# A four-layer transformer kernel on one core: x turned on TensorE instead of in the DMA, and some reciprocals spread over the partitions through DRAM

## The chip, the cores and the metric

The kernel runs on one core of one Trainium2 chip. A core has a matrix engine (TensorE, PE in the profile; PEld is its weight load), a vector engine (VectorE, DVE), an activation engine (ScalarE, ACT), GpSimd (POOL), a sync engine (SP) that here only issues transfers, and 16 DMA engines. SBUF is the working memory with 128 partitions, PSUM takes what TensorE writes in 8 banks of 512 floats per partition, and DRAM lies outside. The metric is the device time of one execution in microseconds (us).

## The reference

Input x has 2048 tokens of 1024 features in bf16. Four layers follow: A, B, A, B. Each is a residual: x = x + layer(normalise(x)). The normalisation takes mean and variance over the features, without weights. There are 32 heads of 32 features.

- Layer A is linear attention. q, k, v come from one weight matrix. q and k are multiplied per head by a 32 x 32 matrix `w_phi`; phi of the result p is softmax(p) and softmax(-p) side by side (64 features). Per head, kv is the sum over all tokens of phi_k times v, and z the sum of phi_k. The output is (phi_q kv) / (phi_q z + 1e-6), and it goes through the matrix `wo`.
- Layer B is full softmax attention with 32 heads over 2048 x 2048 scores, then its own `wo`.

```
pq = einsum(q, w_phi); phi_q = [softmax(pq), softmax(-pq)]      # and phi_k alike
kv = einsum(phi_k, v);  z = sum(phi_k)
o  = (phi_q @ kv) / (phi_q @ z + 1e-6);  x = x + o @ wo          # layer A
o  = softmax(q k^T / sqrt(32)) @ v;      x = x + o @ wo          # layer B
```

## The kernel before

**Layout.** x is kept turned in SBUF for the whole run as `xT`: features on the partitions, tokens along the free side, eight blocks of 128 features by 2048 tokens. The tokens are worked in four chunks of 512 (c = 0 to 3). A group g stands for 128 features, four heads.

**Planner.** The program is not written in its order. The builder makes a list of operations (`op` and `dma`), each with an engine, a duration in the planner's reckoning, the operations it depends on, its buffers and a priority; `Sched.run` then plays them out in a simulated time and gives the order in which they are emitted. Smaller priority numbers come first. A transfer is reckoned to land 2 us plus its `kb`/200 after its issue, where half of the second part also holds up the transfers behind it (`RING`), plus a `slack` of its own. Buffers lie in one SBUF arena (`SBUF_ARENA` bytes per partition) and in the PSUM banks; `QUOTA` says how many of a class may live at once. `TIE` seeds a small random change of the reckoned durations. Many constants are due times (`LATER`, `VQ`, `KP`, `OUT`, `QA`, `AK`, `EARLY` and more), which shift the priority of a piece of work. Each engine takes its instructions in the emitted order.

**Start.** `load_x` brings x. Chunk 0: blocks 0 to 3 by four transposing transfers on SP's queue, blocks 4 to 7 by two plain transfers on POOL's queue into `xnat`, 16 products with the identity on TensorE, and two copies out of PSUM on VectorE. Chunks 1 to 3 come by transposing transfers on SP. `fold_phi` folds `w_phi` into the key weights: weights come plainly (`wnat`, first half by one 1 MB transfer on ACT's queue, second half by four on SP's), TensorE turns them (line 748), four heads at a time are multiplied by the block-diagonal `phi` (line 530, tile `phi_t`), and ACT and VectorE copy the result to a slab (lines 781 and 784). The query weights are folded later, from transposing transfers. `phi_t` is a tile of its own, zeroed by the first instruction of VectorE and filled by four transfers on POOL's queue (line 1380).

**Layer A.** `layernorm` squares x (lines 635 on VectorE for the first chunk, 640 on ACT), sums over the features with a matrix of ones on TensorE (line 602 or 530), spreads the means (line 619) and normalises on VectorE (lines 683 to 695). `a_keys` makes phi_k and v per 128 tokens and sums kv and z over all four chunks. Then `a_queries` runs for each chunk and each half of the heads (hf): query products (530), two exponentials (951), sums over each softmax (962), logarithms, their difference and exponential (968 to 974: the ratio of the two softmax sums, called w here), w spread to all partitions and multiplied onto the second half (979), numerators (994, copied by ACT in 1002), denominators (1009), and the reciprocal of the denominators by logarithm and exponential (1014, 1016). The reciprocal has one useful row per head: rows 32a to 32a+3 hold four heads of group a. `split_hl` splits it on VectorE into a bf16 part and a remainder (915, 916), `spread` multiplies with the 0/1 matrix `selr` on TensorE so that each row fills 32 partitions (931), and line 1020 multiplies the numerators with the spread reciprocal out of PSUM into `oc`. `selb` does the same for w. `a_out` multiplies with `wo` and adds to `xT` (1033). The first of the chunk's later work is planned so that the next chunk's queries come between.

**Layer B.** `attention` computes scores (1257) in groups of three 128 x 512 units, takes the exponential on ACT (1273), and multiplies with v and with ones (1305). For some pairs of units (`COUNT`, `PAIRS`, `HOST`) `exp_dve` computes the exponential on VectorE in six instructions (1184 to 1203); its buffers are `x` (class xy), `z` (xz), `u` (xx) and `y` (xu). The denominators take a way through DRAM: 1362 stores the reciprocals to `rd`, 1364 reads them back with each of four rows broadcast to 32 partitions. Projections for later groups (`b_k`, `b_v`, `b_q`, `b_o`) fill TensorE between. Near the end of the first layer B the keys of the second layer A begin.

Of the kernel before, what the change touches and what calls it, by code (L numbers as in the profile page):

```python
# [55 lines left out]
TIE = 17  # L56
# [13 lines left out]
class Sched:  # L70
# [99 lines left out]
    def run(self):  # L170
# [32 lines left out]
        while left:  # L203
# [108 lines left out]
SBUF_ARENA = 172 * 1024 - 256  # L312
# [3 lines left out]
LONG = {"kT", "v", "slab", "slabk", "xn", "xn1", "kvacc", "kvm", "zm", "wnat"}  # L316
MODEST = {"slabk", "xn1", "e1", "vp1", "pkf", "lnw1", "w2o"}
NUMS = 2
LATER = ((26.4, 16.7, 25.9, 7.3), (18.7, 27.9, 15.9, 13.5))
VQ = (((0, 7.1), (50.5, 3.1), (53.0, 8.9)), ((15.5, 8.4), (75.8, 14.1), (152.2, 9.9)))  # L320
FULL = 5
OUT = (35.9, 27.1)
EARLY = (2.0, 4.0)
DUE = 0.0
BOOST = 25.0
EVAC = 30.0
QA = (105.3, 4.5)
# [4 lines left out]
         "rs": 8, "pkf": 1, "cden": 2, "part": 8, "w2r": 1,  # L332
# [8 lines left out]
HOST = ((), (16,), (11, 17), (0, 11, 21), (4, 10, 17, 24))  # L341
SIDE = (2, 4)
FEW = (((0, 1, 3), (0, 1, 2)), ((0, 1, 3), (0, 1, 2)))
WHOLE = 2
WK = (0.0, 1.5)
SLABD = (1, 3)
TOK = (0.0, 0.6, 0.61, 0.62)
SLOW = 6.0
HALF = 4
KGAP = (6.2, 2.2)  # L350
LATE = 15.3
KP = (0, 39.1, 45.7, 92.0, 62.9, 125.6, 160.1, 205.2)
BO = 225
OP0 = (240.8, 265.9, 289.4)
OGAP = (2.0, 2.6, 1.9)
COUNT = ((0, 0, 1, 2, 4, 4, 4, 3, 4, 3, 3, 4, 4, 4, 4, 3, 4, 3, 3, 4, 3, 2, 1, 2, 0, 2, 4, 2, 1, 2, 3, 3),
    (2, 4, 5, 4, 4, 4, 3, 5, 4, 4, 4, 4, 4, 4, 5, 4, 3, 5, 4, 4, 4, 4, 4, 4, 4, 2, 5, 4, 3, 1, 4, 4))
PAIRS = ((), ((0, 2),), ((0, 2), (1, 2)), ((0, 1), (0, 5), (1, 3)), ((0, 1), (0, 5), (1, 1), (1, 5)),
    ((0, 1), (0, 3), (0, 6), (1, 1), (1, 5)), ((0, 1), (0, 3), (0, 6), (1, 1), (1, 3), (1, 6)))
AK = ((0, 201.9), (1, 231.9), (2, 260.5))  # L360
OUT1 = ((177.6, 3.1), (195.5, 1.0), (246.4, 1.0))


def act_us(n):
    return n / 1200 + 0.064
# [10 lines left out]
def kernel(  # L376
# [52 lines left out]
    phi_t = const.tile([P, G * P], BF16, tag="phi")  # L429
    nc.vector.memset(phi_t[:].bitcast(U32), 0)  # L430
# [45 lines left out]
    gone = []  # L476
    qd = dram_p.tile([P, 2 * G * C512], BF16, tag="qd")
# [78 lines left out]
    def load_x():  # L556
        nb, nv = sb("xnat", TB, C512)
        nat = [dma(-24.0, lambda h=h: nc.gpsimd.dma_start(
            out=nv()[:, 2 * h:2 * h + 2, :],
            in_=A_x[0, 2 * h * P:2 * h * P + 2 * P, C512:D].rearrange("(t p) f -> p t f", p=P)),  # L560
            (), [nb], q="GQ", kb=256, issue=0.75) for h in range(2)]
        for lo, hi, prio, us, kb in ((0, 1, -24.0, 1.3, 128), (1, 2, -9.0, 1.3, 400), (2, NC, -8.0, 2.0, 800)):
            last = []
            for po in range(PO if lo else PO // 2):
                last.append(dma(
                    prio, lambda lo=lo, hi=hi, po=po: nc.sync.dma_start_transpose(
                        out=xT[:, po, lo * C512:hi * C512], in_=A_x[0, lo * C512:hi * C512, po * P:(po + 1) * P]),
                    issue=us, kb=kb))
                if not lo:
                    last[-1].slack = 0.5  # L570
            for pr in () if lo else ((4, 5), (6, 7)):
                tb, tv = ps("wt", ANY)

                def tr(pr=pr, tv=tv, h=0):
                    o = tv().bitcast(BF16)
                    for po in pr:
                        for t in (2 * h, 2 * h + 1):
                            nc.tensor.transpose(
                                out=o[:, (po % 2 * TB + t) * P:(po % 2 * TB + t + 1) * P],
                                in_=nv()[:, t, (po - 4) * P:(po - 3) * P], identity=ident[:])  # L580
                t1 = None
                for h in range(2):
                    t1 = op("PE", 4 * 0.11, lambda tr=tr, h=h: tr(h=h), [nat[h], t1], [tb, nb], -17.0, mode="n")
                last += [op("DVE", 0.69, lambda pr=pr, tv=tv: nc.vector.tensor_copy(
# [1008 lines left out]
```

## Time and profile before

| what | value |
|---|---|
| median of 3 runs | 2245.05 us (2242.07 to 2246.89) |
| profiled execution, its time | 2247.36 us |
| its span, first to last instruction | 2245.1 us |
| granted TensorE clock, mean | 0.998 |
| busy: PE, ACT, DVE, POOL | 2176.1, 1985.7, 1855.9, 197.0 us |
| exponentials of layer B on ACT (line 1273) | 1366 instructions, 1668.5 us |
| the same on VectorE (line 1203, one per pair of units) | 209 instructions, 254.7 us |
| DMA moved | 119.67 MB |

A row of a group has line, engine, operation, the tiles written and read, shape, count, then busy time and mean duration in ns, then idle time of the engine just before and what ended it. PE's busy time counts overlapping matmuls once; it does not say that the matmuls run at their best rate. A row of the timeline has start and duration in us, engine, line, operation and count. SPq, POOLq and ACTq are the queues in which an engine issues transfers. In the table by stage, each engine has its busy time and instruction count.

### The profile page before, as it was taken

The numbers are of one execution on the slowest core, as the hardware profiler recorded it, in microseconds if no ns is written. First come the engines' busy times: TensorE is split into PE (matmuls) and PEld (weight loads), VectorE is DVE, ScalarE is ACT, GpSimd is POOL, SyncE is SP. The second block draws the span as 40 slices with busy tenths as digits, with TensorE's granted clock in tenths as the row PEclk, the third lists the DMA queues.
The fourth block names the chain that finished last, engine by engine and source line by source line (L and its number), as shares of the span: only waits on it lengthen the run. The fifth ranks groups of instructions, "written<-read, shape, count | busy, mean of one in ns | idle before, by whom it ended". The sixth has DMA issues, their size and how long they took to land.

```text
span 2245.1 us, 82636 instructions
## 1 busy us (share of the span) xinstructions
PE 2176.1 (97%) x36788; PEld 872.2 (39%) x36788; DVE 1855.9 (83%) x2761; ACT 1985.7 (88%) x1939; POOL 197.0 (9%) x299
## 2 busy tenths in 40 slices
PE   7999999999999999999999999999999999999999
PEld 4554454444333333333333444433333333333333
DVE  7986873698899889677887788799999999988968
ACT  4436669999999999999998555999999999999998
POOL 1110000000001010121124200000000000100000
PEclk9999999999999999999999999999999999999999
DMA  9220101111122221222235100111111100211111
GB/s 207 49 81 3 33 24 42 41 34 34 51 57 88 74 73 54 64 96 73 78 110 152 59 5 10 36 37 38 36 29 29 35 24 19 73 31 35 47 36 38
DMA packets 121789, 119.67 MB, mean 53 GB/s; under 512 B 57752, under 2 KB 99800, under 8 KB 121432
## 3 DMA queue, kind: packets, MB, share of 16 engines
q1 hardware_dynamic: 102392, 56.64, 10.0%
q0 software_dynamic: 17424, 56.18, 8.7%
q8 instruction: 287, 4.70, 0.9%
q10 hardware_dynamic: 1616, 1.57, 0.2%
q14 instruction: 70, 0.57, 0.1%
HBM read 79.23 MB, written 14.14 MB: 42 GB/s over the span
## 4 chain that ended last, share of the span: by engine, by line
PE 28%; ACT 23%; DVE 9%; issue 5%; DMA 1%; SPq 0%; ACTq 0%; DVEq 0%
ACT arena L1273 22%; PE psum L530 14%; PE psum L1305 6%; PE psum L1257 6%; DVE arena L1203 2%; DVE arena L1184 1%; DVE arena L1196 1%; DVE arena L1201 1%; DVE arena L1193 1%; ACT arena L823 1%; DMA arena<-arena 1%; DVE arena L1370 1%; DVE arena L1198 1%; DVE arena L1057 1%; PE psum L994 0%
## 5 line engine op out<-in xcount | busy, mean ns | idle before, releaser
L1273 ACT ACTIVATE arena<-psum 128x1536 bf16<-128x1536 f32 (+1 forms) x1366 | 1668.5, 1446 | 12.0 <-PE psum L1257 7.1
L530 PE MATMUL psum<-arena 128*32 128x512 bf16 (+1 forms) x18432 | 1058.3, 358 | 12.5 <-DVE arena L836 2.7
L530 PEld LDWEIGHTS <-arena 128*32 128x32 bf16 x18944 | 459.8, 96 | 447.2 <-issue 175.7
L1305 PE MATMUL psum<-arena 128*32 128x512 bf16 x4096 | 628.1, 383 | 4.0 <-issue 2.0
L1305 PE MATMUL psum<-arena,ones_bf 128*32 128x512 bf16 x4096 | 628.1, 383 | 0.0
L1257 PE MATMUL psum<-arena 32*128 32x512 bf16 x4096 | 536.2, 383 | 27.2 <-ACT arena L1273 22.4
L1257 PEld LDWEIGHTS <-arena 32*128 32x128 bf16 x4096 | 158.4, 91 | 555.8 <-issue 549.0
L1184 DVE TENSOR_SCALAR arena<-psum 128x512 int32<-128x512 f32 x418 | 284.5, 686 | 101.7 <-PE psum L1257 90.3
L1203 DVE SCALAR_TENSOR_TENSOR arena<-arena 128x1024 int16<-128x1024 int32 x209 | 254.7, 1218 | 5.7 <-DVE arena L1201 0.4
L1305 PEld LDWEIGHTS <-arena 128*32 128x32 bf16 x4096 | 163.2, 95 | 227.8 <-issue 177.0
L1305 PEld LDWEIGHTS <-ones_bf 128*32 128x32 bf16 x4096 | 161.3, 95 | 22.3 <-issue 7.9
L705 POOL DMA_DIRECT2D arena<-in_B_wqkv_dram x46 | 42.2, 919 | 1248.6 <-PE psum L530 302.5
L1193 DVE TENSOR_SCALAR arena<-arena 128x1024 f16<-128x1024 int16 x209 | 143.8, 690 | 4.4 <-DMA arena<-arena 0.3
L1196 DVE TENSOR_TENSOR arena<-arena 128x1024 f16<-128x1024 f16 x209 | 142.6, 684 | 4.6
L1201 DVE TENSOR_TENSOR arena<-arena 128x1024 f16<-128x1024 f16 x209 | 142.6, 684 | 3.1
L1057 DVE CAST arena<-psum 128x512 bf16<-128x512 f32 x128 | 87.7, 685 | 57.6 <-PE psum L530 57.3
L823 ACT ACTIVATE arena<-psum 128x512 bf16<-128x512 f32 x80 | 43.0, 596 | 82.6 <-PE psum L530 66.7
L827 DVE TENSOR_REDUCE arena<-arena 128x32 f32<-128x1024 bf16 x64 | 77.0, 1214 | 33.3 <-ACT arena L823 33.2
L530 PE MATMUL psum<-xT,onesD 128*32 128x512 bf16 x1144 | 103.1, 381 | 1.3 <-DVE arena L836 0.7
L1321 DVE COPY arena<-psum 128x512 f32<-128x512 f32 x126 | 86.3, 685 | 15.4 <-PE psum L1305 15.0
L1198 DVE TENSOR_SCALAR arena<-arena 128x1024 f16<-128x1024 f16 x209 | 87.9, 422 | 1.7
L836 DVE TENSOR_TENSOR arena<-psum,arena 128x1024 bf16<-128x1024 f32 x64 | 77.4, 1219 | 13.3 <-PE psum L530 9.7
(124 smaller groups left out, 1383.6 us busy)
## 6 DMA issues: line engine op xcount, KB each, us to landing
arena<-rd SPq DMA_DIRECT2D x62, 256.0 KB
arena<-in_B_wqkv_dram POOLq DMA_DIRECT2D x58, 256.0 KB, 4.1
arena<-in_B_wo_dram POOLq DMA_DIRECT2D x40, 256.0 KB, 4.4
arena<-arena SPq DMA_DIRECT2D x256, 32.0 KB
arena<-wd_k POOLq DMA_DIRECT2D x32, 256.0 KB, 5.0
arena<-in_A_wqkv_dram POOLq DMA_DIRECT2D x32, 256.0 KB, 4.6
arena<-arena SPq DMA_DIRECT2D x96, 64.0 KB
arena<-arena SPq DMA_DIRECT2D x248, 2.0 KB
```

Of the source, the lines that this page charges most:

```text
L530: nc.tensor.matmul(out_[ks, :], lhsT=lhsT[:, ks], rhs=rhs, start=start, stop=stop, tile_position=(0, 32 * k), skip_group_check=True)
L1057: return op("DVE", dve_us(512), lambda: nc.vector.tensor_copy(out=dst(), in_=src()), [dep], bufs, prio)
L1184: o = op("DVE", dve_us(512), lambda: nc.vector.tensor_scalar(out=x_v()[:, k, :].bitcast(I32), in0=s_v()[:, x * C512:(x + 1) * C512], scala ...
L1193: last = op("DVE", 1024 / 1920 + 0.15, lambda: nc.vector.tensor_scalar(out=z(), in0=x_v().bitcast(I16).rearrange("p a (n two) -> p a n two ...
L1196: last = op("DVE", 1024 / 1920 + 0.15, lambda: nc.vector.tensor_tensor(out=u(), in0=z(), in1=z(), op=ALU.mult), [last], [z_b, u_b], prio + ...
L1198: last = op("DVE", 1024 / 3840 + 0.15, lambda: nc.vector.tensor_scalar(out=u(), in0=u(), scalar1=POW2_C[0], scalar2=POW2_C[1], op0=ALU.mul ...
L1201: last = op("DVE", 1024 / 1920 + 0.15, lambda: nc.vector.tensor_tensor(out=u(), in0=z(), in1=u(), op=ALU.mult), [last], [z_b, u_b], prio + ...
L1203: return op("DVE", dve_us(1024), lambda: nc.vector.scalar_tensor_tensor(out=y_v().bitcast(I16), in0=x_v().bitcast(I32), scalar=128.0 / BIT ...
L1257: nc.tensor.matmul(out=s_v()[:, x * C512:(x + 1) * C512], lhsT=kT[g][1]()[r, pp, d * P:(d + 1) * P], rhs=q_of[(qc, g)][1]()[r, (pp + j // ...
L1273: ex = op("ACT", act_us(w * C512), lambda s_v=s_v, e_v=e_v, w=w: nc.scalar.activation(out=e_v(), in_=s_v()[:, 0:w * C512], func=ACT.Exp, s ...
L1305: nc.tensor.matmul(out=a_v()[col:col + 32, :], lhsT=v_v()[:, kc % 4, o:o + DH] if what == 0 else ones_bf[:], rhs=ev()[:, x * C512:(x + 1) ...
L1321: cp = op("DVE", dve_us(512), lambda t_v=t_v, a_v=a_v: nc.vector.tensor_copy(out=t_v(), in_=a_v()), [last], [a_b, t_b], prio - 4)
```

## The change

- `load_x`: chunk 0 of x comes by four plain transfers of 256 KB on SP's queue, 128 tokens each; TensorE turns all eight blocks (32 products with the identity) into four PSUM banks, and VectorE and ACT copy two banks each to `xT`. Chunks 1 to 3 are as before.
- `fold_phi`: the first half of the key weights comes by four transfers on SP's queue behind x instead of one on ACT's.
- `phi` becomes a buffer of the arena, zeroed by a planned operation (behind VectorE's constants), and the arena grows by those 2 KB.
- `carry` is new. For the reciprocals of layer A's second and third chunk (`WIRE`, both layers, both halves) it stores the four useful rows of each group to DRAM (`wd`, four transfers of 8 KB) and reads them back with each row broadcast to 32 partitions (seven transfers, 1 MB together, four buffers `wb`, the rows turned round by a per group, as `selr` did). The two VectorE operations of `split_hl` and the products with `selr` fall away for these, and line 1020's product reads SBUF. The ratio w goes by `selb` as before.
- `exp_dve`: `u` and `y` share one buffer (class xx goes).
- Due times and counts change throughout; `EARLY` (first chunk only) becomes `EAR` per chunk and half. `COUNT` adds up to 88 pairs in the first layer B (86 before) and 123 in the second (123).

```diff
-SBUF_ARENA = 172 * 1024 - 256
+SBUF_ARENA = 173 * 1024 + 768
-LATER = ((26.4, 16.7, 25.9, 7.3), (18.7, 27.9, 15.9, 13.5))
+LATER = ((19.6, 38.4, 23.0, 20.6), (36.6, 33.2, 22.3, 16.4))
-OUT = (35.9, 27.1)
-EARLY = (2.0, 4.0)
+OUT = (26.1, 26.4)
+WIRE = (((), (1, 2)), ((), (1, 2)))
+WIRE_SLACK = 1.0
+EAR = ((4.2, 1.9, 5.5, 10.9, 6.1, 10.6, 10.5, 6.6), (0.0, 3.7, 4.6, 9.8, 2.7, 5.5, 7.5, 12.6))
...
-    phi_t = const.tile([P, G * P], BF16, tag="phi")
-    nc.vector.memset(phi_t[:].bitcast(U32), 0)
...
     def load_x():
-        nb, nv = sb("xnat", TB, C512)
...
+        nb, nv = sb("xnat", TB, D)
+        nat = [dma(-24.0, lambda t=t: nc.sync.dma_start(out=nv()[:, t, :], in_=A_x[0, t * P:t * P + P, :]),
+                   (), [nb], kb=256) for t in range(TB)]
+        first = []
+        banks = [ps("wt", ANY) for _ in range(4)]
+        turned = [None] * 4
+        for t in range(TB):
+            for i, (tb, tv) in enumerate(banks):
+                def tr(i=i, t=t, tv=tv):
+                    o = tv().bitcast(BF16)
+                    for po in (2 * i, 2 * i + 1):
+                        nc.tensor.transpose(
+                            out=o[:, (po % 2 * TB + t) * P:(po % 2 * TB + t + 1) * P],
+                            in_=nv()[:, t, po * P:po * P + P], identity=ident[:])
+                turned[i] = op("PE", 2 * 0.11, tr, [nat[t], turned[i]], [tb, nb], -17.0, mode="n")
...
-            ld.append([dma(-24.0, lambda: nc.scalar.dma_start(out=nv()[:, :, 0:C512], in_=A_w[:, :, col:col + C512]),
...
+            for h in range(2):
+                ld.append([dma(-22.0 + 2 * h, lambda h=h, i=i: nc.sync.dma_start(
+                    out=nv()[:, 2 * i:2 * i + 2, C512 * h:C512 * h + C512],
+                    in_=A_w[:, 2 * i:2 * i + 2, col + C512 * h:col + C512 * h + C512]),
+                    (), [nb], kb=256) for i in range(4)])
...
+    def carry(r_b, r_v, dep, prio, turn):
+        at_d = wd_v[len(sent)]
+        sent.append(prio)
+        st = [dma(prio, lambda a=a: nc.sync.dma_start(out=at_d[a], in_=r_v()[32 * a:32 * a + 4, :]),
+                  [dep], [r_b], kb=8) for a in range(4)]
+        got = []
+        for a in range(4):
+            b, v = sb("wb", C512, dt=F32)
+            got.append((b, v, [st[a], b, v]))
+        r = []
+        for a, (b, v, _) in enumerate(got):
+            n = turn * a % 4
+            for lo, hi, to in ((0, 4 - n, n), (4 - n, 4, 0)):
+                if hi > lo:
+                    o = dma(prio, lambda a=a, v=v, lo=lo, hi=hi, to=to: nc.sync.dma_start(
+                        out=v()[32 * to:32 * (to + hi - lo), :],
+                        in_=at_d[a, lo:hi].unsqueeze(1).to_broadcast([hi - lo, 32, C512])), [st[a]], [b], kb=260 * (hi - lo))
+                    o.slack = WIRE_SLACK
+                    r.append((a, o))
+        return [(b, v, [o for x, o in r if x == a]) for a, (b, v, _) in enumerate(got)]
...
-        k_b, k_v, k = split_hl(r_b, r_v, l4, prio)
-        for a, (b_, v_, bm) in enumerate(spread(k_b, k_v, k, prio, selr)):
+        if c in WIRE[layer][1]:
+            wide_ = carry(r_b, r_v, l4, prio, 1)
+        else:
+            k_b, k_v, k = split_hl(r_b, r_v, l4, prio)
+            wide_ = spread(k_b, k_v, k, prio, selr)
+        for a, (b_, v_, bm) in enumerate(wide_):
...
-        u_b, u_v = sb("xx", 2, C512)
         y_b, y_v = sb("xu", 2, C512)
+        u_b, u_v = y_b, y_v
...
+    phi_b, phi = sb("phi", G, P)
+    phi_0 = op("DVE", 0.5, lambda: nc.vector.memset(arena[:, phi_b.at // 2:phi_b.at // 2 + G * P].bitcast(U32), 0),
+               (), [phi_b], -30.0)
...
-                a_queries(c, hf, pr + 5 * hf, wq_s, state, oc, EARLY[layer] if c == 0 else 0.0)
+                a_queries(c, hf, pr + 5 * hf, wq_s, state, oc, EAR[layer][2 * c + hf])
```

More of the change, by code (lines that the diff above doesn't have):

```diff
@@ L568, in load_x @@
                     issue=us, kb=kb))
[L569 to L584, printed above, removed]
-                    out=xT[:, pr[0]:pr[1] + 1, 0:C512],
-                    in_=tv().bitcast(BF16).rearrange("p (o n) -> p o n", o=2)), [t1], [tb], -17.0)] * 2
             for c in range(lo, hi):
@@ L722, in slab_turned @@
         return b, v, [o] * 4
-    def phi():
-        return phi_t[:].rearrange("p (g n) -> p g n", g=G)
     def fold_phi(col, wd_v, prio, use_pe):
@@ L975, in a_queries @@
                [df], [lp_b, lm_b], pre)
[L976 removed]
         ew, nums = [], []
[L978 removed]
+        if c in WIRE[layer][0]:
+            wide_ = carry(lm_b, lm_v, w, pre, 0)
+        else:
+            h_b, h_v, h = split_hl(lm_b, lm_v, w, pre)
+            wide_ = spread(h_b, h_v, h, prio, selb)
+        for a, (b_, v_, bm) in enumerate(wide_):
             ew.append(op("DVE", dve_us(512), lambda v_=v_, a=a: nc.vector.tensor_tensor(
                 out=eq[a][1]()[:, 1, :], in0=eq[a][1]()[:, 1, :], in1=v_(), op=ALU.mult),
[L981 removed]
+                flat([bm, tot[1]]), [b_, eq[a][0]], pre if c in WIRE[layer][0] else prio))
         d_b, d_v = ps("cmp", ANY)
```

73 lines of the change are left out of this document (36 added, 37 removed), and 1 row of the table QUOTA.

## The prediction

> **What bounds the kernel now.** I read four views in this order: busy time by stage, the groups by shape, the timeline of the start, and short stages around single transfers. First the stages, cut where the work changes; columns are busy microseconds and instructions of PE, PEld, DVE, ACT, POOL, then granted clock, DMA share, GB/s.
>
> ```profile
> 0.00:32.00 32.00, 17.29 (x402) 11.86 (x406) 22.21 (x51) 15.44 (x24) 4.57 (x12) 1.00 0.93 223
> 64.00:140.00 76.00, 72.93 (x1993) 44.31 (x1980) 69.07 (x83) 28.03 (x53) 11.11 (x23) 1.00 0.17 52
> 140.00:327.00 187.00, 186.84 (x3765) 90.39 (x3761) 148.22 (x208) 108.50 (x193) 13.04 (x23) 1.00 0.10 27
> 400.00:1213.00 813.00, 791.86 (x12397) 285.96 (x12397) 669.05 (x990) 805.16 (x685) 119.55 (x168) 1.00 0.25 71
> 1213.00:1416.00 203.00, 200.38 (x4001) 98.61 (x3997) 159.92 (x224) 119.98 (x210) 19.44 (x35) 0.99 0.13 37
> 1416.00:2235.00 819.00, 799.40 (x12135) 289.37 (x12128) 733.28 (x1138) 814.08 (x688) 23.14 (x27) 1.00 0.13 35
> ```
>
> Up to 32 us PE is idle nearly half the time and the DMA engines are full (0.93): the start waits for data. From 64 us layer A fills PE (72.93 of 76), and from 140 to 327 and from 1213 to 1416 it leaves PE next to no gap (186.84 of 187, 200.38 of 203): a microsecond of PE work taken out there is a microsecond of time. From 400 to 1213 and from 1416 to 2235, layer B runs, and ACT has no gap (805 of 813, 814 of 819): only less work on ACT, or a better use of its 8 and 5 idle us, shortens these. PE is nearly full there too, but with waits of its own inside. The stages follow each other, so gains add.
>
> **The start.** The timeline (start, duration, engine, line, operation, idle before it and its releaser):
>
> ```profile
> 0.75 5.34 SPq L566 DMA_TRANSPOSE xT<-in_A_x_dram  x4
> 0.77 0.46 ACTq L732 DMA_DIRECT2D arena<-in_A_wqkv_dram  x1
> 1.47 1.56 POOL L558 DMA_DIRECT2D arena<-in_A_x_dram  x2 [0.17 <-issue]
> 3.03 2.33 POOL L1380 DMA_DIRECT2D phi_t<-in_A_w_phi_dram  x4
> ...
> 5.45 0.15 DVE L463 TENSOR_SCALAR hl<-hl 128x1 f32<-128x1 f32 x1
> ...
> 11.73 1.46 PE L578 MATMUL psum<-ident,arena 128*128 128x128 bf16 x12 [2.81 <-DMA arena<-in_A_x_dram]
> ...
> 12.04 0.69 DVE L635 TENSOR_TENSOR arena<-xT 128x1024 bf16<-128x1024 bf16 x1 [6.44 <-DMA xT<-in_A_x_dram]
> 12.65 0.68 DVE L584 COPY xT<-psum 128x1024 bf16<-128x1024 bf16 x1
> ...
> 16.56 0.63 PE L602 MATMUL psum<-arena,onesD 128*32 128x512 bf16 x2
> ...
> 18.99 0.74 PE L530 MATMUL psum<-phi_t,arena 128*32 128x128 bf16 x32
> ...
> 31.31 7.28 PE L530 MATMUL psum<-arena 128*32 128x512 bf16 x128
> ```
>
> DVE waits 6.44 us for x and can square it only at 12.04; the sums of the first normalisation end at 17.2 (16.56 + 0.63); the steady stream of key products begins at 31.31. What kept x away is seen in the DMA of 2 us stages:
>
> ```profile
> 2.00:4.00 2.00, 0.00 (x0) 0.00 (x0) 1.70 (x11) 0.02 (x1) 2.00 (x4) 1.00 0.96 293
> ...
> 8.00:10.00 2.00, 0.61 (x4) 0.34 (x4) 0.00 (x0) 0.00 (x0) 0.00 (x0) 1.00 1.04 99
> ...
> 14.00:16.00 2.00, 2.00 (x19) 1.32 (x17) 2.00 (x4) 1.01 (x1) 0.00 (x0) 1.00 1.12 334
> ...
> 22.00:24.00 2.00, 1.79 (x61) 1.28 (x50) 2.00 (x4) 2.00 (x5) 0.00 (x0) 1.00 0.60 139
> ...
> 30.00:32.00 2.00, 1.79 (x72) 1.31 (x75) 2.00 (x4) 1.16 (x4) 0.00 (x0) 1.00 1.09 381
> ```
>
> While the plain 1 MB load of the ACT queue ran, the engines moved 293 GB/s; at 8 to 10 us, when the four transposing loads were left beside POOL's plain x, they were as full and moved 99; plain weight loads then got 334.
>
> The change replaces the four transposing loads and POOL's half of x by four plain loads, first in SP's queue. *Early end:* 512 rows of 2 KB, 1.05 MB, at 293 GB/s from 2.0 us is landed at 5.6; the last block's 8 transposes take 1.0 us (1.46 for 12), two copies on DVE, with two on ACT beside them, 1.4 (2 x 0.68), four squares 2.8 (4 x 0.69), the last sums 0.6. They end at 11.4, 5.8 us sooner. *Late end:* x lands as POOL's did, 8.1 us (median) after issue:
>
> ```profile
> arena<-in_A_x_dram POOLq DMA_DIRECT2D x2, 256.0 KB, 8.1
> phi_t<-in_A_w_phi_dram POOLq DMA_DIRECT2D x4, 16.0 KB, 8.8
> ```
>
> that is 1.5 + 8.1 = 9.6, and the sums end at 15.4: 1.8 us sooner. Two things pull against it. The weights' first half leaves the ACT queue for SP behind x, so it lands 3.6 us after x, at 9.2 or later: time enough, as the fold began at 18.99. And phi's zeroing now stands behind DVE's constants (end 5.6) instead of ahead of them, so its four loads issue from 6.1 instead of 3.03; with the same 8.8 us the last lands at 16.7 (6.1 + 1.8 + 8.8), and the fold, which began at 18.99, gains only 2.3. Their queue no longer has 512 KB of x ahead, so I expect them sooner. From 22 to 32 DVE has no gap (2.00 of 2), so its work shifts whole, and the stages behind, PE 72.93 of 76 busy, carry the gain on. Ends: 0 (something else late) and 5.8; I take **4.0**, nearer to the row of the hardware queue than to POOL's. PE's 16 further transposes (2 us) lie in its idle time; without that they would cost 2 us.
>
> [...]
>
> **The reciprocals.** Of two chunks of four, in both layers A, the two DVE operations that split the reciprocal, and the products by `selr` that spread it, go (8 times):
>
> ```profile
> L931 PE MATMUL psum<-arena,selr 32*128 32x512 bf16 x32 | 4.2, 384 | 0.0
> L915 DVE CAST arena<-arena 128x512 bf16<-128x512 f32 x16 | 6.8, 424 | 13.5 <-ACT arena L1016 13.4
> L916 DVE SCALAR_TENSOR_TENSOR arena<-arena,hl 128x512 bf16<-128x512 bf16 x16 | 12.0, 751 | 0.4
> ...
> L972 DVE TENSOR_TENSOR arena<-arena 128x512 f32<-128x512 f32 x8 | 5.5, 685 | 0.0
> L1020 DVE TENSOR_TENSOR arena<-arena,psum 128x512 bf16<-128x512 f32 x32 | 20.0, 682 | 0.7 <-PE psum L931 0.6
> ```
> ```profile
> L931 PE MATMUL psum<-arena,selr 32*128 32x512 bf16 x32 | 3.8, 384 | 0.0
> ```
>
> PE: half of 4.2 and half of 3.8 = **4.0 us** off a full PE. DVE: 8 x (0.424 + 0.751) = 9.4 us, worth nothing, for DVE was busy 148 of 187; were DVE the bound it would be up to 9.4 more. The final product reads SBUF instead of PSUM: 685 against 682 ns, nothing.
>
> Added are 4 small stores and 7 broadcast loads (1 MB) on SP each time. Their price in time is bounded by the one broadcast load of 256 KB that layer B makes; its store issued at 864.48, the load at 865.95:
>
> ```profile
> 864.48 0.33 SPq L1362 DMA_DIRECT2D rd<-arena  x1
> 865.95 0.58 SPq L1364 DMA_DIRECT2D arena<-rd  x1
> ```
> ```profile
> 867.00:868.00 1.00, 0.81 (x15) 0.29 (x7) 0.87 (x2) 1.00 (x2) 0.00 (x0) 1.00 0.17 59
> 868.00:869.00 1.00, 1.00 (x19) 0.44 (x20) 1.00 (x2) 1.00 (x2) 0.00 (x0) 1.00 0.26 102
> 869.00:870.00 1.00, 0.73 (x15) 0.19 (x3) 1.00 (x2) 1.00 (x2) 0.11 (x1) 1.00 0.24 94
> ```
>
> It keeps a quarter of the DMA engines at work for 2.7 us. Four of these one behind another take 11; with 1.5 us from store to load and 1.3 to the first data, the last lands some 14 us after the reciprocal. The planner's own formulas in the code reckon 2.6 for a store, 16 rows x 0.65 on the ring, 2 and 1 of slack: 16, so the products are planned late enough. In order of time, before:
>
> ```profile
> 225.14 0.66 ACT L1016 ACTIVATE arena<-arena 128x512 f32<-128x512 f32 x1
> ```
> ```profile
> 227.62 2.48 DVE L1020 TENSOR_TENSOR arena<-arena,psum 128x512 bf16<-128x512 f32 x4
> ...
> 240.84 0.69 DVE L1033 TENSOR_TENSOR xT<-xT,psum 128x512 bf16<-128x512 bf16 x1
> ```
>
> Now the products follow the reciprocal (end 225.8) by 1.8 us; the output projection that needs them evacuates first at 240.8, 15 us after it, since the next chunk's queries come between. That is the cover, and it is just enough; without it PE would wait up to 12 us each time. I take **0**.
>
> [...]
>
> SP's issues, 8 x (4 x 0.33 + 7 x 0.58) = 43 us, fall in stages of 187 and 203 us where the DMA is nearly idle (share 0.10 and 0.13); if its queue were not, the moves of keys would queue behind them.
>
> **The rest.** `COUNT` sends 88 pairs instead of 86 past ACT in the first layer B, and 123 as before in the second. Groups by shape:
>
> ```profile
> L1273 ACT ACTIVATE arena<-psum 128x1536 bf16<-128x1536 f32 x946 | 1317.1, 1573 | 9.5 <-PE psum L1257 6.4 <-PE psum L1305 1.6 <-DVE arena L1203 0.5
> L1273 ACT ACTIVATE arena<-psum 128x1024 bf16<-128x1024 f32 x420 | 433.2, 1158 | 2.6 <-PE psum L1305 0.8 <-PE psum L1257 0.7 <-issue 0.5
> ```
>
> A wide exponential keeps ACT 1.39 us (1317.1/946), a narrow one 1.03; a pair narrows two: 4 x 0.36 = **1.4 us** off ACT; DVE has 144 idle us there. `u` over `y`, phi in the arena, and the new due times (`EAR`, `LATER`, `VQ`, `KP` and others) move work within full stages: nothing, between a gain of the 13 us that ACT idles and a like loss.
>
> **Sum.** 4.0 + 4.0 + 1.4 = 9.4. The profiled execution took 2247.4 (span 2245.1), so 2238.0; it lay 2.3 above the median of 2245.05, so I forecast 2235.6, rounded to 2236.
>
> **Rivals.** *A, the start keeps its length:* phi or the weights behind x are late by as much as x is early, or bytes and not transposes set the start. Then 5.4 remain: 2239.7. For it: phi's 16.7; against: the 99 GB/s. [...] *B, the broadcast loads come too late (slower):* the four products wait in DVE's order, and behind them the next half's products and the residual adds that free PSUM, so PE stops. 1.2 us of PE lost per spread cancels all (9.4/8); if other loads share that quarter of the engines, 2.5 us too late each time costs 8 x 2.5 = 20 less a fifth that DVE idles, 16: 2252. For it: 14 us of transfer, from one row, against a cover of 15; against: the planner's 16. [...] *C, the new order loses elsewhere what is won* (attention starts later, or ACT's idle 13 us grow by 9): 2245. *D, the new order also fills ACT's idle time by half, 6.5:* 2229.
>
> **Chances.** Forecast 0.50, A 0.17, B 0.13, C 0.12, D 0.08. What this kernel's timing can tell from no change is about 0.2%, 4.5 us. Faster by more holds for the forecast nearly always (0.46), half of A (0.10) and D (0.08), with a little of C: 0.66. Within it: the rest of A, most of C: 0.20. Slower: B and a little: 0.14. The range goes from 2226 (the start at its early end gives 1.8 more, part of D the rest) to 2248 (C, and the edge of B); the forecast's own is 2230 to 2241.
>
> **What would show it.** Right: L635's first square near 8 us instead of 12.04, the stream of 128 key products near 27, the first exponential 6 us sooner; `selr` in 16 matmuls a layer instead of 32; layer A's second stage 2 us shorter; 1 to 2 us less ACT in the first layer B. Wrong: a wait on phi at the fold, DVE waits of over 1 us for DMA at L1020's successor, PE gaps in 140 to 327, ACT idle over 13 us.

## The result and the profile after

The changed kernel takes 2266.26 us (median of 4 runs, 2264.16 to 2267.57) against 2245.97 for the kernel before on the same chip: a ratio of 1.0085, with a 95% interval of 1.007 to 1.0099. By the ratio it is slower by some 19 us, where 9 less was forecast. The profiled execution took 2265.0, its span 2262.9.

The layers B hardly moved; the two layers A did. From the first and the last exponential of each layer B, in us:

| | before | after |
|---|---|---|
| first exponential of the first layer B | 327.1 | 334.3 |
| first layer B, first exponential to last | 885.6 | 885.0 |
| second layer A, last exponential to first | 199.8 | 207.8 |
| second layer B | 822.4 | 825.3 |

So +7.2, -0.6, +8.0 and +3.0, in one trace each. Busy time by stage, cut as in the prediction (busy us and instructions of PE, PEld, DVE, ACT, POOL, then granted clock, DMA share, GB/s):

```profile
0.00:32.00 32.00, 23.56 (x478) 16.05 (x479) 24.98 (x55) 19.54 (x27) 3.47 (x11) 0.89 1.02 233
64.00:140.00 76.00, 74.81 (x1892) 45.84 (x1895) 69.07 (x80) 28.30 (x52) 11.21 (x23) 0.98 0.18 52
140.00:327.00 187.00, 178.48 (x3526) 86.53 (x3522) 139.41 (x195) 102.95 (x182) 13.19 (x23) 0.99 0.17 50
400.00:1213.00 813.00, 790.90 (x12427) 282.85 (x12424) 675.28 (x1007) 805.76 (x688) 118.81 (x165) 1.00 0.24 69
1213.00:1416.00 203.00, 193.35 (x3711) 91.44 (x3707) 150.83 (x211) 116.69 (x199) 19.23 (x36) 0.99 0.20 62
1416.00:2235.00 819.00, 798.94 (x12281) 293.53 (x12277) 734.86 (x1139) 808.71 (x692) 25.04 (x29) 1.00 0.13 35
```

Up to 32 us PE does 6 us more than before. But from 140 to 327 and from 1213 to 1416, where it had next to no gap (0.2 and 2.6 us), it now idles 8.5 and 9.7 us: the two stages lose 15.4 us of PE, and the two layers A are 15.2 longer. The granted clock has little part in it: 0.99 and 0.99 there, where it was 1.00 and 0.99. The groups by shape say who waits for what there (busy us, mean ns, then idle time before them and its releasers):

```profile
L1048 DVE TENSOR_TENSOR arena<-arena 128x512 bf16<-128x512 f32 x32 | 22.1, 690 | 32.2 <-DMA arena<-wd__120 31.8
L1048 DVE TENSOR_TENSOR arena<-arena,psum 128x512 bf16<-128x512 f32 x32 | 19.9, 683 | 2.4 <-PE psum L930 2.4
L930 PE MATMUL psum<-arena,selr 32*128 32x512 bf16 x32 | 3.5, 384 | 0.0
L914 DVE CAST arena<-arena 128x512 bf16<-128x512 f32 x24 | 10.2, 423 | 17.3 <-ACT arena L1040 15.7 <-ACT arena L994 1.6
L1301 ACT ACTIVATE arena<-psum 128x1536 bf16<-128x1536 f32 x942 | 1313.3, 1549 | 11.8 <-PE psum L1285 8.4 <-PE psum L1333 1.5 <-DMA arena<-arena 1.1
L1301 ACT ACTIVATE arena<-psum 128x1024 bf16<-128x1024 f32 x424 | 437.1, 1130 | 3.7 <-PE psum L1333 2.0 <-PE psum L1285 0.9 <-DVE arena L1398 0.4
```

The first row is the carried kind of final product (L1048; L1020 before): 690 ns each, as forecast, but 31.8 us of waiting for the broadcast loads, in 8 spreads 4.0 us each. The other kind, fed from PSUM, waits 2.4. `selr` is down to half, and a quarter of the splits (L914) is gone.

One chunk of the first layer A, on the timeline (start, duration, engine, line, operation, idle before it and its releaser). L1040 is the reciprocal, L939 the stores, L950 the broadcast loads:

```profile
210.31 0.63 ACT L1040 ACTIVATE arena<-arena 128x512 f32<-128x512 f32 x1
213.05 0.63 ACT L1040 ACTIVATE arena<-arena 128x512 f32<-128x512 f32 x1
...
218.88 0.69 DVE L1048 TENSOR_TENSOR arena<-arena 128x512 bf16<-128x512 f32 x1
218.95 3.22 SPq L939 DMA_DIRECT2D wd__120<-arena  x4
...
221.77 0.69 DVE L1048 TENSOR_TENSOR arena<-arena 128x512 bf16<-128x512 f32 x1 [2.19 <-DMA arena<-wd__120]
227.06 0.69 DVE L1048 TENSOR_TENSOR arena<-arena 128x512 bf16<-128x512 f32 x1 [1.84 <-DMA arena<-wd__120]
...
229.97 4.89 SPq L950 DMA_DIRECT2D arena<-wd__120  x7
...
237.43 6.48 PE L533 MATMUL psum<-arena 128*32 128x512 bf16 x104
...
243.43 0.69 DVE L1048 TENSOR_TENSOR arena<-arena 128x512 bf16<-128x512 f32 x1 [2.35 <-DMA arena<-wd__120]
...
246.19 0.69 DVE L1048 TENSOR_TENSOR arena<-arena 128x512 bf16<-128x512 f32 x1 [0.87 <-DMA arena<-wd__120]
246.94 0.40 PE L533 MATMUL psum<-arena 128*32 128x512 bf16 x4 [2.36 <-DVE arena L1048]
```

The reciprocals of a chunk's two halves end at 210.94 and 213.68, 2.7 us apart; before they were 17 apart. The first half's third product gets its data at 227.06, 16.1 us after the reciprocal, the fourth goes at 229.77, 18.8 after it. The second half's stores go out at 218.95, when SP has issued the first half's loads, and its own loads only at 229.97, 11 us behind the stores: SP waits there for the stores to land (5.4 us of it at one instruction). Its third product starts at 243.43, 29.8 after its reciprocal. In stages of 3 us around it:

```profile
235.00:238.00 3.00, 3.00 (x60) 1.71 (x56) 2.94 (x3) 2.89 (x7) 0.00 (x0) 1.00 0.31 91
238.00:241.00 3.00, 3.00 (x53) 1.26 (x42) 2.91 (x4) 0.58 (x2) 0.00 (x0) 1.00 0.18 68
241.00:244.00 3.00, 2.82 (x52) 1.41 (x48) 0.66 (x2) 0.00 (x0) 0.00 (x0) 1.00 0.13 51
244.00:247.00 3.00, 0.46 (x8) 0.17 (x11) 2.13 (x5) 1.23 (x2) 0.00 (x0) 1.00 0.09 29
```

While DVE waits for the last pieces, the DMA is at 0.13 of its 16 engines, some 2 (the 0.09 is two more microseconds at 0.13 and 0.14, and one without traffic); and PE, which had no gap here before, works 0.46 of 3 us. Why so little of the DMA works on these pieces is not shown: no view names the engines of a piece. The prediction had the last load land some 14 us after the reciprocal; in the second layer A a fourth product still waits 2.1 us for its load and goes 18.2 after its reciprocal.

The start, on the timeline:

```profile
0.75 1.81 SPq L561 DMA_DIRECT2D arena<-in_A_x_dram  x4
...
5.70 2.45 POOL L1411 DMA_DIRECT2D arena<-in_A_w_phi_dram  x4 [4.39 <-DVE arena L1409]
...
6.99 0.62 PE L571 MATMUL psum<-ident,arena 128*128 128x128 bf16 x8 [0.50 <-DMA arena<-in_A_x_dram]
...
8.51 2.49 DVE L639 TENSOR_TENSOR arena<-xT 128x1024 bf16<-128x1024 bf16 x4
...
13.35 0.39 PE L606 MATMUL psum<-xT,onesD 128*32 128x512 bf16 x2
...
14.52 0.35 PE L533 MATMUL psum<-arena 128*32 128x128 bf16 x12 [0.22 <-ACT arena L755]
...
25.26 0.60 ACT L822 ACTIVATE arena<-psum 128x512 bf16<-128x512 f32 x1 [0.75 <-PE psum L533]
```

The first square starts at 8.51 (12.04 before), the fold at 14.52 without a wait for phi (18.99), the first key exponential at 25.26 (31.37). This 6 us lead then melts: at the end of the first chunk's keys it is 3.3, at the first reciprocal 2.2 (182.2 against 184.4). The second number can't be read closely: eight of the traces here, of this kernel and of the experiments below, have the same order of work up to the first reciprocal and have it begin at 180.7 to 184.6, in the mean 0.9 us sooner than the one trace of the kernel before.

### The profile page after: what moved, and what is told of

Its sections match the earlier page's. It is cut to its first block, busy times and chain, and to the rows that moved or that the text cites. A ratio compares the mean times of both kernels' runs of the same rounds, so it can differ in the third digit from the quotient of the medians.

```text
span 2262.9 us, 82808 instructions
## 1 busy us (share of the span) xinstructions
PE 2181.9 (96%) x36816; PEld 876.0 (39%) x36816; DVE 1854.0 (82%) x2759; ACT 1990.1 (88%) x1941; POOL 196.8 (9%) x297
## 3 DMA queue, kind: packets, MB, share of 16 engines
q1 hardware_dynamic: 106600, 66.87, 11.4%
## 5 line engine op out<-in xcount | busy, mean ns | idle before, releaser
L1301 ACT ACTIVATE arena<-psum 128x1536 bf16<-128x1536 f32 (+1 forms) x1366 | 1666.1, 1419 | 15.4 <-PE psum L1285 9.3
L533 PE MATMUL psum<-arena 128*32 128x512 bf16 (+2 forms) x18944 | 1071.0, 354 | 25.8 <-issue 6.7
L1285 PEld LDWEIGHTS <-arena 32*128 32x128 bf16 x4096 | 153.3, 91 | 551.6 <-issue 543.5
```

The source lines that it names most:

```text
L533: nc.tensor.matmul(out_[ks, :], lhsT=lhsT[:, ks], rhs=rhs, start=start, stop=stop, tile_position=(0, 32 * k), skip_group_check=True)
L1285: nc.tensor.matmul(out=s_v()[:, x * C512:(x + 1) * C512], lhsT=kT[g][1]()[r, pp, d * P:(d + 1) * P], rhs=q_of[(qc, g)][1]()[r, (pp + j // ...
L1301: ex = op("ACT", act_us(w * C512), lambda s_v=s_v, e_v=e_v, w=w: nc.scalar.activation(out=e_v(), in_=s_v()[:, 0:w * C512], func=ACT.Exp, s ...
```

## The experiments

Throughout, a wait means idle time before an instruction. A single trace places a stage to about 4 us only, as those eight show; one kernel profiled twice, below, has its first layer B begin at 325.2 and 322.0. The times over several runs carry the verdicts (two runs only for the products planned later, the new start alone, and one-row loads in the first halves). The theory at the outset, theory 1 below, was rival B of the prediction: the broadcast loads land late, and DVE, in its order, waits for them. The rivals to it were that the re-drawn order of work is to blame, and the new start.

**One-row loads.** Each broadcast load is cut into rows; 16 loads of 64 KB stand for 7 of 64 to 256 KB. Order of work on PE, DVE and ACT as in the changed kernel.

```
-            n = turn * a % 4
-            for lo, hi, to in ((0, 4 - n, n), (4 - n, 4, 0)):
+            for lo in range(4):
+                hi, to = lo + 1, (lo + turn * a) % 4
```

> The changed kernel in its own order, with one edit: every broadcast load of the carry brings one row to 32 partitions (16 loads instead of 7, the planner reckons the same landing). [...] Theory 2 (the new due times are bad in themselves, whatever the loads do): waits fall but the time stays within 5 us of 2266. Theory 3 (any way through DRAM is too late): the products still come 15 us or more after the reciprocal and the time stays.

2239.15 us, ratio 0.9959 (0.9945 to 0.9973): faster than the kernel before, and by 0.0126, some 28 us, than the changed kernel in its own order. The groups of this kernel:

```profile
L1048 DVE TENSOR_TENSOR arena<-arena 128x512 bf16<-128x512 f32 x32 | 21.8, 684 | 8.5 <-DMA arena<-wd__120 8.5
```

and its stages of 3 us at the same point:

```profile
235.00:238.00 3.00, 3.00 (x63) 1.37 (x52) 3.00 (x4) 2.97 (x7) 0.00 (x0) 1.00 0.41 109
238.00:241.00 3.00, 3.00 (x63) 2.45 (x57) 3.00 (x4) 1.08 (x2) 0.00 (x0) 1.00 0.33 73
241.00:244.00 3.00, 3.00 (x61) 2.27 (x56) 3.00 (x7) 1.23 (x2) 0.00 (x0) 1.00 0.16 44
244.00:247.00 3.00, 2.94 (x55) 1.72 (x49) 3.00 (x6) 0.00 (x0) 0.00 (x0) 1.00 0.18 44
```

The wait for loads falls from 31.8 to 8.5 us and PE works through. The gain is more than the 14 to 20 us that theory 1 gave this run, though the waits are over the 3 us a layer that it allowed. The stores of a second half no longer hold up its loads (1.7 to 1.9 us between their issues, where it was 11 to 12). More than twice the loads of the same bytes come sooner, so neither bytes nor SP's issues were the limit in the changed kernel. What differs is how much of the DMA was at work: in the first three of these stages 0.41, 0.33 and 0.16 of it, where it was 0.31, 0.18 and 0.13. Why larger pieces keep less of it at work is not shown.

**No carry at all**, the rest of the change kept.

```
-WIRE = (((), (1, 2)), ((), (1, 2)))
+WIRE = (((), ()), ((), ()))
```

> The changed kernel without the carry: all reciprocals spread by TensorE as before, start and due times as changed. The order is planned anew, which by itself can move the whole by some 10 us, so layer A's two stages are to be compared, not the whole alone. Theory 1 (late loads): no waits for these loads, TensorE without gaps over 0.5 us in the layer-A stages except a few us; first exponential at 326 to 330 instead of 334, second layer A 200 to 203 us instead of 208. Theory 2 (due times): layer A's stages stay as long as in the changed kernel, 334 and 208.

2254.35 us, 1.0031 (1.0019 to 1.0043). Without the carry, 12 us of the loss go, but not all. The first exponential of layer B comes at 328.0, as theory 1 had it; the second layer A lasts 206.1, nearer to the 208 of theory 2 than to the 200 to 203 of theory 1. The order is drawn anew, and in it the rest (start, due times, counts) does not win by itself: by the prediction's terms it should be 5.4 us faster (4.0 + 1.4), and it is 7 slower.

**The products planned later.**

```
-WIRE_SLACK = 1.0
+WIRE_SLACK = 6.0
```

> The changed kernel with 6 us instead of 1 of slack in the planner's reckoning for the carry's loads; the loads themselves as they are. Theory 1 with its second half (what costs is that VectorE's order has the products too early): VectorE's waits for these loads fall from 16 us to under 6 in each layer A, TensorE's gaps to half, and the layer-A stages get shorter by 3 to 6 us each (first exponential 328 to 331, second layer A 202 to 205). Rival (the late products themselves hold up the output projection, whatever the order): waits go, but the gaps move to the output projection and the stages stay within 2 us of 334 and 208.

2260.15 us, 1.0056 (1.0036 to 1.0076). The waits for loads are all but gone:

```profile
L1048 DVE TENSOR_TENSOR arena<-arena 128x512 bf16<-128x512 f32 x32 | 21.9, 683 | 1.0 <-DMA arena<-wd__120 1.0
```

yet two thirds of the loss stay: a layer A still ends late (first exponential at 332.5, as the rival had it; second layer A 205.2, at the edge of theory 1). So DVE's standing may not be all that costs: the products come late in this order too, and what needs them with them. This order is a new draw as well, so the run can't tell the two apart.

**The new start alone**, in the kernel before: `load_x`, weights and phi as changed, all times and counts of before (and 2 KB more of arena, for phi).

```
...
-    phi_t = const.tile([P, G * P], BF16, tag="phi")
...
-        for lo, hi, prio, us, kb in ((0, 1, -24.0, 1.3, 128), (1, 2, -9.0, 1.3, 400), (2, NC, -8.0, 2.0, 800)):
+        nat = [dma(-24.0, lambda t=t: nc.sync.dma_start(out=nv()[:, t, :], in_=A_x[0, t * P:t * P + P, :]),
+                   (), [nb], kb=256) for t in range(TB)]
...
```

> The kernel before with the new start alone (x and the key weights loaded plainly on SP's queue, x turned by TensorE, phi in the arena, which grows by 2 KB). Theory: the first normalisation is 5 us earlier, and 2 us of that are left when the keys of the last chunk end (172.8 instead of 174.8), as in the changed kernel. Rival (the gain at the start is lost by the next waits whatever follows): under 0.7 us left there. Later stages are planned anew and can differ by several us either way.

2274.15 us, 1.0118 (1.0098 to 1.0138): the slowest of all, though its first chunk of keys ends 1.9 us sooner (61.9 against 63.8). The keys of the last chunk, expected 2 us sooner, end 1.8 us later (176.6 against 174.8). By number that is the rival's case, but one trace can be off by more than the 2 us in question. Its first layer B lasts 892.7 and its second layer A 212.8, 7 and 13 us longer. The new start touches neither. I put it down to the order, drawn anew with due times set for the old start; that is argued, not shown.

**Which half of the carry is late?** One-row loads only in the first halves, then only in the second halves.

```
-            for lo, hi, to in ((0, 4 - n, n), (4 - n, 4, 0)):
+            for lo, hi, to in ([(k, k + 1, (k + n) % 4) for k in range(4)] if len(sent) % 2 == 1 else ((0, 4 - n, n), (4 - n, 4, 0))):
```

(for the second halves, `== 0`)

> The changed kernel, in which only the first half of each of the two chunks (heads in the first four rows of chunks 1 and 2, both layers A) brings its reciprocals with one-row loads; the second halves keep pieces of four, three, two and one rows. In the changed kernel the products of a first half began up to 1.8 us and those of a second half up to 5.3 us later than they were planned. Theory Q: the second half is late because its stores and loads queue behind the first half's pieces on the same two to four DMA engines; then the first half's short loads clear the way for both, and this kernel gives at least two thirds of the 27 us (0.0126) that one-row loads everywhere gave: ratio 0.9995 or less against the kernel before. Rival O: each half waits for its own pieces only; then it gives the smaller part, a third or less: 1.004 or more.

> The mirror of it: only the second halves have one-row loads; the planned order of work on PE, DVE and ACT is that of the changed kernel, instruction for instruction. [...] Rival O: two thirds or more: 0.9995 or less.

First halves: 2261.42, 1.007 (1.0044 to 1.0096). Second halves: 2252.13, 1.0024 (1.0014 to 1.0034). The groups, of the first halves' kernel:

```profile
L1048 DVE TENSOR_TENSOR arena<-arena 128x512 bf16<-128x512 f32 x32 | 21.9, 688 | 18.8 <-DMA arena<-wd__120 16.7 <-issue 2.0
```

and of the second halves':

```profile
L1048 DVE TENSOR_TENSOR arena<-arena 128x512 bf16<-128x512 f32 x32 | 22.0, 688 | 19.4 <-DMA arena<-wd__120 19.3
```

In the wait rival O is right: each half waits for its own pieces. Added up over its rows in the timelines, the idle time before the carried products is 20.5 us for the first halves and 11.7 for the second in the changed kernel; 7.7 and 11.1 with quick loads in the first halves; 19.4 and 0 with quick loads in the second. So the second half isn't late only through the first. (Theory Q's two to four engines are an estimate, 0.13 to 0.26 of 16; that both halves' pieces are on the same ones is not shown.) In time neither theory's numbers are met by both runs: the second halves, in the same order as the changed kernel, give 0.0061 of the 0.0126, where theory Q had a third or less and rival O two thirds or more, and the first halves 0.0015, but there the planner moved other work from the middle of the first layer A on, so that number isn't theirs alone. The three kernels of one order are the clean series: 31.8, 19.3 and 8.5 us of waiting, and 1.0085, 1.0024 and 0.9959. Each microsecond of waiting less is worth about 1.2 us (28 over 23.3); why a little more than itself is not shown.

**What is a re-drawn order worth?** The number that draws the planner's ties is exchanged: 17 for 22 in the kernel with one-row loads, 22 for 17 in the kernel before.

```
-TIE = 22
+TIE = 17
```

> One-row loads everywhere, with the number that draws the planner's ties set back from 22 to 17, so that only the order of work within the stages differs. If the gain over the kernel before (0.9959) comes from what is computed and loaded, it stays within 0.3% of it: 0.993 to 0.999. If the order that was drawn decides, the ratio may fall anywhere between 0.99 and 1.01, and the stages may each move by 5 us or more.

> The kernel before with that one number set from 17 to 22 and nothing else: the same work, another order. It shows what a re-drawn order alone is worth. If little, 0.998 to 1.002 and each stage within 2 us of the kernel before (first exponential of layer B 327.1, attention 885.6 and 822.4, second layer A 199.8). If the kernel before owes its time to its drawn order, some 0.5% slower, with stages that differ by 5 us and more.

2252.07, 1.0029 (1.0016 to 1.0041), where 0.9959 was the same work in the other order: outside the 0.993 to 0.999 expected if the draw did not matter. And 2249.9, 1.0018 (1.0006 to 1.003), for the kernel before, with its first exponential of layer B 3.0 us later and the other stages within 2. The draw alone moves the time by 0.2 to 0.7%; the prediction's whole sum is 0.4%.

**What are the start and the PE work worth, in one order?** One-row loads as the base, once more; the base with x and the weights made late by a 1 MB copy ahead of them; and the base with the `selb` products of the two chunks done four times over.

```
...
+            if not t:
+                nc.sync.dma_start(out=spare[:], in_=A_x[0, C512:2 * C512, :])
+            nc.sync.dma_start(out=nv()[:, t, :], in_=A_x[0, t * P:t * P + P, :])
```
```
-                for k in range(2):
+                for k in [0, 1] * times:
...
-            wide_ = spread(h_b, h_v, h, prio, selb)
+            wide_ = spread(h_b, h_v, h, prio, selb, 4 if c in WIRE[layer][1] else 1)
```

> One-row loads everywhere, unchanged, as the base of the two runs after it, on one chip with them: 0.9959 as before, within 0.0015. If its gain lay in that chip alone, nearer to 1.

> One-row loads everywhere, and a copy of 1 MB from DRAM to DRAM ahead of x in SP's queue; every instruction of PE, DVE and ACT and its order stay. It makes x, and the weights behind it, late by some 4 to 8 us (the first square, at 8.5 us, shows by how much) and so asks what a microsecond of the start is worth at the end. Theory K (the start is kept): the stages behind are full, so the first exponential of layer B and the end come later by the same amount, 4 us or more. Theory L (the start is lost on the way, as the gain of 6 us at the first key exponential had shrunk to 2.2 by the first reciprocal): a third to a half of it, 1.5 to 3 us.

> One-row loads everywhere, and in chunks 1 and 2 of both layers A each product by selb that spreads a weight is done four times instead of once, with the same result; order and all else stay. That adds 96 of the matmuls of which the change removed 32 (4.0 us), so 12 us of PE, 6 a layer. Theory: PE sets the length of layer A, so the time grows by 9 to 12 us, 4.5 to 6 in each layer A, and the removal of the 32 was worth 3 to 4. Rival: PE has slack beside these chains (waits on loads, on DVE): the time grows by 4 us or less, and the removal was worth 1 or nothing.

The base: 2242.13, 0.9978 (0.9968 to 0.9987), still faster than before, but by less than on the first chip, and outside the 0.0015 expected; against the changed kernel's 1.0085 it puts the worth of one-row loads at 24 us (0.0107) instead of 28. x late: 2242.97, 0.9981 (0.9972 to 0.9991). More PE work: 2243.82, 0.9985 (0.9976 to 0.9995). Against the base of the same chip, 10 runs each, the means differ by 0.6 us (-1.4 to 2.5) and 1.5 us (-0.3 to 3.2), with 95% intervals. What was added is seen on the timeline, of the base:

```profile
8.92 2.49 DVE L639 TENSOR_TENSOR arena<-xT 128x1024 bf16<-128x1024 bf16 x4
```

of the kernel with x late:

```profile
11.07 2.49 DVE L645 TENSOR_TENSOR arena<-xT 128x1024 bf16<-128x1024 bf16 x4
```

and in the groups, of the base and of the kernel with four times the products:

```profile
L930 PE MATMUL psum<-arena,selb 32*128 32x512 bf16 x64 | 8.8, 383 | 0.3 <-DVE arena L915 0.3
```
```profile
L930 PE MATMUL psum<-arena,selb 32*128 32x512 bf16 x160 | 14.9, 378 | 0.0
```

x was late by 2.2 us, not the 4 to 8 expected. Its trace ends the first chunk's keys at 63.0, where the eight traces without the copy have 59.8 to 61.5, but at the first reciprocal (183.1) and at the first exponential of layer B (325.1; 325.2 and 322.0 without the copy) it lies among them. At the end at most 2.5 are left. Theory L fits, K isn't excluded. The 96 added products cost 6.1 us of busy PE (14.9 - 8.8), not 12, since the repeats overlap (each lasts some 378 ns and adds 64 ns of busy PE); and of these 6.1 the time shows 1.5, between none and half, as the rival had it. So taking out the 32 `selr` products, 4 us by their row, was worth an estimated 1 us (4 x 1.5 / 6.1), some 2 at most; they stand elsewhere in the order than the `selb` products, so this is no measurement of them.

**The carry alone, by one-row loads**, in the kernel before: the `carry` function and its uses, nothing else.

```
+        if c in WIRE[layer][1]:
+            wide_ = carry(r_b, r_v, l4, prio, 1)
+        else:
...
```

> The kernel before with the reciprocals of chunks 1 and 2 carried through DRAM by one-row loads, and nothing else of the change: start, due times and counts of before, but the planner draws another order. The carry in good time is worth 4 us of PE at most, so 0.998, give or take the 0.003 that a re-drawn order has shown. If the carry costs even when its loads are one row each, 1.003 and more, with DVE's waits at the final product over 3 us a layer.

2261.98 us, 1.0064 (1.0049 to 1.0079). Both signs of a carry that costs came: over 1.003, and over 3 us of DVE's waits for loads a layer, 9.5 in all. But the one-row kernel in the changed order waits as long (8.5 and 9.9 in its two traces) and is faster than the kernel before, so the waits don't explain the 14 us; the first layer B lasts 894.5 (885.6) and the second layer A 205.8 (199.8). As with the start alone, the order is drawn anew with times set for another program; that this is the reason is argued, not shown. What the carry is worth without that stays open.

## Why the prediction was wrong

**The step that failed** is the price of the broadcast loads in *The reciprocals*, "I take 0", resting on a cover of 15 us against a transfer of 14. Both numbers were wrong. The transfer: 14 us was four loads of 256 KB at the rate of one such load of layer B, and the last pieces, of fewer rows, kept 0.13 of the DMA engines at work instead of 0.24 to 0.26; a first half's third product gets its data 15 to 16 us after the reciprocal, and the fourth, in the two cases where it waited, 18.2 and 18.8 after it.

For the second half the sum's "1.5 us from store to load" was 11 to 12, and its stores first had to wait for SP to issue the first half's loads: its third product starts 26 to 30 us after its reciprocal. In the changed kernel the reciprocals of a chunk's halves lie 2.7 to 5 us apart, where it was 14 to 17 before; the prediction had no term for this. It takes the new due times (`EAR` among them) and the carry together: the kernel without the carry has 9 to 12, and the kernel before with the carry 9 to 11. The spacing alone does not cost the time: the kernel with one-row loads has the same and is faster than the kernel before.

The cover: 15 us was the distance to the output projection *before*. But DVE, which takes its work in order, stands at the products themselves and not at the projection: in the changed order it comes to the second one 8.6 us after the reciprocal (221.77 - 2.19 against 210.94), and everything else of DVE is behind it. By the planner's own 16 us "the products are planned late enough"; its formula, 0.65 us of ring for each 260 KB times four, knows neither the share of the DMA that a load keeps at work nor the wait for stores.

That this step is what cost the time is shown by the kernel with one-row loads, of the same order instruction for instruction on PE, DVE and ACT: 23.3 us less of waiting, some 28 us less time.

**Rival B was the right mechanism at too low a price**, and got 0.13. It had the products waiting in DVE's order, PE stopping behind them and the slower side: all seen. It had 2.5 us late each time and 16 us of loss; measured are 4.0 (31.8/8) and 24 to 28 (0.0107 and 0.0126). Of the prediction's signs of being wrong three came: DVE's waits of over 1 us at these products, PE's gaps from 140 to 327, and ACT idle over 13 us (9.3 and 7.3 in the two layers B).

**The start, 4.0 us.** Its early part was right: x lands near the 293 GB/s end (last transposes at 6.99), squares at 8.51 for "near 8", the first exponential 6 us sooner. The sums end at 13.7, between the two ends of 11.4 and 15.4; phi, feared for 16.7, was no hindrance. (The transposing loads read rows of 256 bytes and the plain ones of x whole rows of 2 KB; no run tells whether the turning or the short rows kept the DMA at 99 GB/s, where plain loads moved 293 and 334.) What most likely failed is "the stages behind carry the gain on": of 6 us some 0.9 is left at the first reciprocal, in the mean of eight traces, and 2.2 us of x taken away again cost 0.6 at the end (2.5 at most). The term was worth perhaps 1; that is argued from these two numbers, not measured.

**PE's 4.0 us.** The row was read rightly (7.9 to 3.5 in the two layers together) but "a microsecond of PE work taken out there is a microsecond of time" does not hold: about a quarter of it does, half at most, by the run with four times the products. My reading, not shown: the planner fills PE with whatever is at hand, so a full PE isn't yet the chain that ends the stage, which runs through normalisations and reciprocals too.

**`COUNT`, 1.4 us.** The counts came as read (946 and 420 to 942 and 424), and so did ACT's work. From first to last exponential, the first layer B before and after:

```profile
327.10:1212.70 885.60, 863.44 (x13693) 317.46 (x13685) 695.02 (x1025) 877.10 (x746) 122.92 (x171) 1.00 0.24 68
```
```profile
334.30:1219.30 885.00, 860.83 (x13697) 314.40 (x13691) 699.08 (x1039) 875.75 (x746) 125.96 (x175) 1.00 0.24 69
```

ACT is busy 1.4 us less, but the layer is only 0.6 shorter, for ACT idles 9.3 us in it instead of 8.5. (The two rows by shape, 1313.3 and 437.1 us, don't show the gain: exponentials of different shapes overlap and are counted in both, and the rows add up to 1750.4 where the line's busy time is 1666.1.) The second layer B is 3.0 longer, and ACT's idle time in it is up from 5.0 to 7.3; why is not shown.

**The due times, priced at 0 between -13 and +13.** No run has the due times alone. But the same work in another draw differs by 11 to 16 us (1.0029 against 0.9978 and 0.9959), about as much as these bounds, so a sum of 9.4 us of small terms can't be told from the draw.

That the sum came close to the truth once the loads were quick (9.1 us and 5.4 gained on two chips, by the medians) is chance: its terms are each smaller, and the draw is in it.

## What to carry to other kernels

Where a kernel waits for loads that spread a few rows over the partitions, try them in smaller pieces: here the same bytes in 16 transfers of one row times 32 partitions, instead of 7 of one to four rows, were worth 24 to 28 us. Before an added wait is called covered, look where the waiting instruction stands in the *new* order and what else the same change sends down the same queue at that moment. And where a planner redraws the order, measure what a draw alone is worth first: terms below that size can be tried only in a fixed order.

## What the runs showed of the hardware

Sixteen loads of 64 KB from one queue come sooner than seven of 64 to 256 KB, 1 MB in both cases: of the second half shown above, the fourth product starts at 246.19 in the changed kernel, after a wait of 0.87 us for its load and 16.2 us after the first load's issue (229.97), and at 242.86 with one-row loads, without such a wait and 14.3 us after it (228.58). SP takes the same time for either kind, some 0.7 us each: the kernel of one-row loads issues sixteen in 11.14 us, and the changed one seven in 4.89. With one-row loads the issue is thus most of the carry:

```profile
215.52 11.14 SPq L950 DMA_DIRECT2D arena<-wd__120  x16
```

The added `selb` products, on different groups of 32 rows, cost 64 ns of busy PE each (6.1 us for 96), against 138 (8.8/64) as they stand in the base, four or two together, though each lasts some 380 ns. And the granted clock was lower for a few microseconds in some traces of an order and not in others. In the changed kernel it was 0.57 here:

```profile
20.00:24.00 4.00, 3.58 (x40) 2.88 (x43) 4.00 (x5) 4.00 (x6) 0.00 (x0) 0.57 0.95 300
```

The kernel with quick loads in the second halves shows 0.58 in the same stage, the kernel before and the one with one-row loads 1.00 there. Such dips are not all of why one trace places a stage only to some 4 us: two traces of the same order without a dip, of the base and of the kernel with more products, differ by 3.0 at the first reciprocal (180.7 and 183.7).
